# Two weight matrices transposed from DRAM, one load for the key, and an inverse Fourier table built by DMA, in a fused layer with its gradients

## The chip, the cores and the metric

The kernel runs on one core of a Trainium2 chip. Its time is the device time of one execution in microseconds (us). Times of several runs are given as a median with the smallest and the largest; a profile is taken from one further execution, whose own time is given beside them.

## The reference

The kernel computes a layer and all of its gradients in one launch. S = 2048 tokens, D = 512 channels, F = 1376 hidden units, all inputs bf16:

```python
def _A_ref(q, k, v, shift_k, ssm_k, ssm_D):      # q is xn here
    k_pad = jnp.pad(k, ((0, 0), (3, 0), (0, 0)))
    k_shift = sum(k_pad[:, t:t+S, :] * shift_k[:, 3-t] for t in range(4))
    kv = k_shift * v
    y  = irfft(rfft(kv, 2*S) * rfft(ssm_k, 2*S))[:S]   # long convolution, per channel
    return q * (y + kv * ssm_D)

def _B_ref(x, w_gate, w_up, w_down):
    return (sigmoid(x @ w_gate) * (x @ w_up)) @ w_down

xn  = layernorm(A_q)
out = A_q + _A_ref(xn, A_k, A_v, ...) * silu(_B_ref(xn, ...))
```

There are ten outputs: out, and with grad_out given the gradients of A_q, A_k, A_v, shift_k, ssm_k, ssm_D, w_gate, w_up and w_down. The input B_x is not used.

## The kernel before

*How the order of the work comes about.* The kernel is written as generators that record operations. A class `Rec` keeps every operation with its operands and dependences; a list scheduler (`order`, L347) then lays them out on the engines with a cost model (`cost` L290 for compute, `dcost` L327 for DMAs), and `emit` issues them in that order. All matmuls therefore have line L544 in the profile and everything else has L546. Each engine works its own list in order, and so do the queues: a DMA that is issued by SyncE (SP) goes to SP's queue, and the same holds for the queues of ScalarE (ACT) and GpSimd (POOL). Buffers are rings in one large SBUF slab (`Ring`, `Arena`), so in the profile nearly every on-chip buffer is called `slab`.

*Forward (about 0 to 208 us).* Three generators are interleaved. `strG` goes over 8 blocks of 256 tokens: load x (`f_x`), layer norm (`f_ln`), transpose of xn (`f_T`, a transposing DMA on SP; block 0 is transposed on TensorE instead), and the gate and up matmuls (`f_gen`), whose sigmoid and h are kept on chip for blocks 6 and 7 and written to DRAM scratch (`sF_d`, `hS_d`) for the others. `strK` transforms the filter ssm_k for four groups of 128 channels with a length-4096 FFT made of matmuls and twiddles. `strV` does, for each channel group, the 4-tap shift on the key as matmuls (`tok`) on a transposed key `kT`, the product with v, the forward FFT, the product with the filter's spectrum, and the inverse (`inv3`, `inv1`, ending in stream transposes on VectorE (DVE)).

The key comes transposed from DRAM in two loads of 256 columns (`ld_kT`, L905), the second recorded at the second channel group (L1009). Tables: `gen_fft_consts` (L576) makes the forward cosine table, a copy of it in DRAM scratch (`Cn_d`) and the twiddles; `gen_inv_table` (L631), called in the first channel group, makes the inverse table `Ci` with integer steps on DVE and two Sin on ACT. The row of shift_k (`skr`) is loaded in the beginning and spread over the partitions by four matmuls with a row of ones (`skb`, L944 to 947). `Dcol_b` (L926) and `skT` (L927) are small loads on ACT's queue that bring ssm_D and shift_k with the channel on the partition.

*Between the passes.* SP's list then holds the loads of w_down (`wd`), its transpose (`wdT`), and the transposes of gate and up:

```python
1071    nc.sync.dma_start_transpose(wdT[:, :, 0:F], B_w_down)
1073    for w, wT in ((wg, wgT), (wu, wuT)):
1074        for db in range(4):
1075            nc.sync.dma_start_transpose(wT[:, :, db * 128:(db + 1) * 128], w[:, db, :])
```

Gate and up are read from their copies in SBUF, 128 rows at a time; these copies are padded from 1376 to FP = 1408 columns with zeros, so a transposed weight has 11 blocks of 128 partitions.

*Backward over token blocks (about 208 to 365 us).* `stepB` (L1157) takes the blocks in the order 6, 7, 0 to 5. For each, `z_gen` (L1085) multiplies h by w_down, makes out and the gradient dz, and transposes dz by a DMA on SP (`dzT`); `d_gen` (L1117) multiplies dzT by `wdT` and makes the gradients of gate and up (`dg`, `du`, also written to scratch); `x_gen` (L1135) multiplies these by `wgT` and `wuT` and finishes the gradient through the layer norm. sigmoid and h of blocks 0 to 5 are loaded again on SP.

*The rest.* Weight gradients (L1195), then per channel group the backward of the long convolution (`frontC` L1247, `backC` L1261). In `backC` DVE makes dks, and two copies inside SBUF move its last rows to other partitions (the carried rows, L1290 and 1291, on POOL's queue) before the 4-tap shift is applied backwards.

Of the kernel before, what the change touches and what calls it, by code (L numbers as in the profile page):

```python
# [16 lines left out]
P = 128  # L17
# [9 lines left out]
NG = 4  # L27
# [135 lines left out]
class Rec:  # L163
# [163 lines left out]
    def dcost(self, alt):  # L327

        eng, meth, a, k = alt
        dst, src = a[0], a[1]  # L330
        nb = math.prod(dst.shape) * esize(dst.dtype)
        if "transpose" in meth:
            return (1.4 if str(src.space) != "DRAM" else nb / 260e3), nb / 256 * 18 / 16e3
        run = 4096 if eng == "sync" else 1 << 13
        for v in (dst, src):
            dims = [d for d in v.ap if d[1] > 1]
            r = 1
            for s, n in reversed(dims if str(v.space) == "DRAM" else [d for d in v.ap[1:] if d[1] > 1]):
                if s != r:
                    break  # L340
                r *= n
            run = min(run, r * esize(v.dtype))
        pk = nb / run
        d = pk * max(8 + 0.0375 * run, 18) / min(16, pk) / 1e3
        return (0.58 + max(0, pk - 256) * 3e-4 if eng == "gpsimd" else 0.36 + max(0, pk - 128) * 6e-4), d

    def order(self):  # L347
# [28 lines left out]
        pipe = {"gpsimd": 0.0, "hw": 0.0}  # L376
# [40 lines left out]
        while ndone < len(ops):  # L417
# [59 lines left out]
            if op.dma:  # L477
                occ, d = self.dcost(alt)
                me, other = ("gpsimd", "hw") if e == "gpsimd" else ("hw", "gpsimd")
                t = max(t, pipe[me] - 12.0)  # L480
                t0 = max(pipe[me], t + 1.5)
                share = min(d, max(0.0, pipe[other] - t0))
                pipe[me] = t0 + d + share
                if share:
                    pipe[other] += share
# [90 lines left out]
def gen_fft_consts(nc, ar, negpi, CN, TT, RT, I32, Cn_d):  # L576
# [8 lines left out]
    nc.gpsimd.iota(a, pattern=[[1, 16]], base=0, channel_multiplier=16)  # L585
    pi_ = tmp([4], i32)
    nc.gpsimd.iota(pi_[:, 0:1], pattern=[[0, 1]], base=0, channel_multiplier=1)
    b = tmp([64], i32)
    nc.gpsimd.iota(b, pattern=[[2, 64]], base=1, channel_multiplier=0)
# [9 lines left out]
    x32 = tmp([32], f32)  # L599
    nc.gpsimd.iota(x32, pattern=[[1, 32]], base=0, channel_multiplier=0, allow_small_or_imprecise_dtypes=True)  # L600
# [28 lines left out]


def gen_inv_table(nc, ar, negpi, Ci):  # L631
    rings = []

    def tmp(shape, dt):
        r = Ring(ar, shape, dt)
        rings.append(r)
        return r.ap
    pk = tmp([1], i32)
    for e in range(2):
        nc.gpsimd.iota(pk[64 * e:64 * e + 64], pattern=[[0, 1]], base=1, channel_multiplier=2)  # L640
    kf = tmp([1], f32)
    nc.vector.tensor_copy(kf, pk)
    nn, mc = tmp([16, 64], f32), tmp([2, 16, 64], i32)
    m = mc[:, 0]
    for h in range(2):
        nc.gpsimd.iota(nn, pattern=[[1, 16], [32, 64]], base=16 * h, channel_multiplier=0, allow_small_or_imprecise_dtypes=True)
        nc.vector.tensor_scalar(m, nn, kf[:, 0:1], None, ALU.mult)
        nc.vector.tensor_single_scalar(mc[:, 1], m, 8191, ALU.bitwise_and)
        nc.vector.tensor_single_scalar(m, m, 6144, ALU.add)
        nc.vector.tensor_single_scalar(mc[:, 0], m, 8191, ALU.bitwise_and)  # L650
        nc.scalar.activation(Ci[:, :, 16 * h:16 * h + 16], mc, ACT.Sin, bias=negpi, scale=2 * math.pi / 8192)
    for r in rings:
        r.free()
# [11 lines left out]
def kernel_impl(ctx, tc, A_q, A_k, A_v, A_shift_k, A_ssm_k, A_ssm_D, B_x, B_w_gate, B_w_up, B_w_down,  # L665
# [49 lines left out]
    Ci = Ring(ar, [2, 32, 64]).ap  # L715
# [32 lines left out]
    def f_T(q):  # L748
        T[q]["xnT"] = xnT_r.next()
        nc.sync.dma_start_transpose(T[q]["xnT"].rearrange("p t b k -> p (t b) k"),  # L750
                                    xnA[:, 2 * q:2 * q + 2, :].rearrange("p t d -> p (t d)"))

# [91 lines left out]
    def inv1(B, dst):  # L844
        for jh in range(2):
            ps = nc.ps("m2", [2, 8, 64], f32)
            calls = []
            for jj in range(8):
                j = 8 * jh + jj
                for c in range(2):  # L850
                    for r in range(2):
                        for e in range(2):
                            h = slice(64 * e, 64 * e + 64)
                            calls.append(("matmul", (ps[64 * r:64 * r + 64, e, jj], Ci[h, c, 16 * r + j, :],
                                                     B[h, c, 16 * r + j].rearrange("p u w -> p (u w)")),
                                          dict(start=(c == 0), stop=(c == 1))))
# [6 lines left out]
    def inv1n(B, dst):  # L863
        ps = nc.ps("f4", [32, 64], f32)
        for jh in range(2):
            for j8 in range(2):
                calls = []
                for jj in range(8 * j8, 8 * j8 + 8):
                    for c in range(2):
                        for e in range(2):  # L870
# [3 lines left out]
                                                     Ci[h, c, j, :]), dict(start=(c == 0), stop=(c == 1))))  # L874
# [120 lines left out]
    def strV():  # L995
        for cg in range(NG):
# [11 lines left out]
            if cg == 1:  # L1008
                ld_kT(1)  # L1009
# [5 lines left out]
            if cg == 0:  # L1015
                gen_inv_table(nc, ar2, negpi, Ci)
# [29 lines left out]

    CN_r.free()
    x2_r, go_r = Ring(ar, [2, D], n=2), Ring(ar, [2, D], n=2)
    dzT_r = Ring(ar, [2, 4, 128], n=2)
    dxa_r = Ring(ar, [2, D], n=2)  # L1050
    wd_r = Ring(ar, [NFB, D])
    zw = {k: Ring(ar, [2, D]) for k in ("sigz", "gate", "s_out", "dgate", "om")}
# [15 lines left out]
    nc.sync.dma_start(wd[0:96, NFB - 1, :], B_w_down[128 * (NFB - 1):F, :])  # L1068
    BQ = list(range(8 - NKEEP, 8)) + list(range(8 - NKEEP))
# [191 lines left out]
    def backC():  # L1261
        for cg in range(NG):
# [27 lines left out]
            nc.gpsimd.dma_start(dks[0:64, NJ:NJ + 3, :], dks[64:128, 0:3, :])  # L1290
            nc.gpsimd.dma_start(dks[64:127, NJ:NJ + 3, :], dks[1:64, 0:3, :])
# [53 lines left out]
    for r in [wd_r, x2_r] + list(zw.values()):  # L1345
# [97 lines left out]
```

## Time and profile before

| what | value |
|---|---|
| time, median of 3 runs (smallest to largest) | 586.28 us (585.12 to 590.41) |
| time of the profiled execution | 581.78 us |
| its span | 580.0 us |
| mean granted TensorE clock | 0.928 |
| PE busy | 485.9 us (84%), 6721 instructions |
| DVE busy | 409.9 us (71%), 625 |
| ACT busy | 273.2 us (47%), 335 |
| POOL busy | 51.9 us (9%), 92 |
| packets | 183,200, of which 112,607 under 512 bytes |
| SP's queue (q1), share of the 16 DMA engines' span | 66.4% |
| POOL's queue (q0) | 13.2% |
| ACT's queue (q10) | 0.1% |
| HBM read and written | 38.97 MB and 47.35 MB, 149 GB/s |

Engines: PE is TensorE's matmul, DVE VectorE, ACT ScalarE, POOL GpSimd, SP SyncE. Busy time counts neither register nor semaphore instructions nor the issuing of DMAs. The table of windows gives for each stretch of the span its length, the busy time of PE, its weight loads, DVE, ACT and POOL with the number of instructions in brackets, the granted TensorE clock, the busy share of the 16 DMA engines and GB/s. A line of the timeline gives start, length, engine, line and operation, output and input by the program's names, how many instructions run together in it, and in square brackets how long the engine stood idle before and what ended this. A line that begins with SPq is a DMA that SP issues.

### The profile page before, as it was taken

The numbers are of one execution on the slowest core, as the hardware profiler recorded it, in microseconds if no ns is written. First come the engines' busy times: TensorE is split into PE (matmuls) and PEld (weight loads), VectorE is DVE, ScalarE is ACT, GpSimd is POOL, SyncE is SP. The second block draws the span as 40 slices with busy tenths as digits, with TensorE's granted clock in tenths as the row PEclk, the third lists the DMA queues.
The fourth block names the chain that finished last, engine by engine and source line by source line (L and its number), as shares of the span: only waits on it lengthen the run. The fifth ranks groups of instructions, "written<-read, shape, count | busy, mean of one in ns | idle before, by whom it ended". The sixth has DMA issues, their size and how long they took to land. (4 is left out here: it accounts for less than half of the span.)

```text
span 580.0 us, 15280 instructions
## 1 busy us (share of the span) xinstructions
PE 485.9 (84%) x6721; PEld 304.7 (53%) x6721; DVE 409.9 (71%) x625; ACT 273.2 (47%) x335; POOL 51.9 (9%) x92
## 2 busy tenths in 40 slices
PE   4385979999599839999999999897687889669986
PEld 2283767887476615544564655343443444345444
DVE  5589988769448369779887698267674995566363
ACT  4369666767325423333453343355562451642412
POOL 6121341112111000000000000000000010000000
PEclk9697998999879878999999999899687899889999
DMA  8923698653949995587685869999569879998735
GB/s 244 278 73 135 197 225 252 186 193 127 258 110 257 234 213 129 172 252 203 188 225 152 254 140 233 247 267 222 164 164 192 177 204 280 231 247 174 178 95 149
DMA packets 183200, 114.93 MB, mean 198 GB/s; under 512 B 112607, under 2 KB 168637, under 8 KB 182110
## 3 DMA queue, kind: packets, MB, share of 16 engines
q1 hardware_dynamic: 175324, 88.59, 66.4%
q0 software_dynamic: 6752, 25.36, 13.2%
q8 instruction: 52, 0.85, 0.6%
q10 hardware_dynamic: 1058, 0.01, 0.1%
q14 instruction: 14, 0.11, 0.1%
HBM read 38.97 MB, written 47.35 MB: 149 GB/s over the span
## 5 line engine op out<-in xcount | busy, mean ns | idle before, releaser
L544 PE MATMUL psum<-slab 64*64 64x64 bf16 (+8 forms) x6712 | 483.5, 260 | 87.5 <-issue 23.7
L544 PEld LDWEIGHTS <-slab 128*128 128x128 bf16 (+6 forms) x6712 | 303.8, 105 | 267.5 <-issue 109.3
L546 ACT CAST slab<-psum 128x1024 bf16<-128x1024 f32 (+3 forms) x236 | 199.1, 891 | 198.1 <-PE psum L544 162.9
L546 DVE TENSOR_TENSOR slab<-slab 128x1024 bf16<-128x1024 bf16 (+4 forms) x317 | 247.9, 814 | 42.6 <-PE psum L544 16.2
L546 ACT ACTIVATE slab<-psum 128x1024 bf16<-128x1024 f32 (+2 forms) x56 | 49.0, 877 | 85.3 <-PE psum L544 76.8
L546 DVE CAST slab<-psum 128x1024 bf16<-128x1024 f32 (+2 forms) x39 | 41.3, 1067 | 46.8 <-ACT slab L546 34.0
L546 DVE SCALAR_TENSOR_TENSOR slab<-slab 128x512 bf16<-128x512 bf16 (+1 forms) x48 | 25.6, 532 | 22.6 <-ACT slab L546 21.9
L546 DVE TENSOR_TENSOR slab<-psum,slab 128x1024 bf16<-128x1024 f32 (+2 forms) x28 | 28.2, 1007 | 18.7 <-PE psum L544 15.8
L546 DVE STREAM_TRANSPOSE slab<-slab 128x512 f32<-128x512 f32 x48 | 31.0, 686 | 10.5 <-ACT slab L546 10.1
L546 DVE TENSOR_SCALAR slab<-slab 128x1 f32<-128x1 f32 (+10 forms) x74 | 28.2, 410 | 8.3 <-DMA slab<-slab 5.8
L546 ACT ACTIVATE slab<-slab 128x512 bf16<-128x512 bf16 (+2 forms) x20 | 19.4, 977 | 16.1 <-DVE slab L546 15.0
L546 POOL DMA_DIRECT2D slab<-slab x8 | 4.3, 544 | 190.8 <-DVE slab L546 190.8
L546 DVE BATCH_NORM_STATS2 slab<-slab 128x6 f32<-128x512 bf16 x16 | 11.0, 685 | 12.2 <-DMA slab<-in_A_q_dram 12.2
L546 POOL MEMSET slab<- 128x128 bf16 (+3 forms) x9 | 3.0, 342 | 166.5 <-issue 165.3
L546 POOL TENSOR_TENSOR slab<-slab 128x1 f32<-128x1 f32 (+1 forms) x20 | 11.4, 573 | 34.4 <-DVE slab L546 34.1
L546 POOL DMA_DIRECT2D KK_d<-slab x16 | 8.8, 547 | 52.1 <-ACT slab L546 45.4
L546 POOL DMA_DIRECT2D hS_d<-slab x8 | 8.8, 1102 | 25.8 <-DVE slab L546 22.9
L546 ACT ACT_TABLE_LOAD x7 | 9.0, 1283 | 3.4 <-issue 2.3
L546 POOL DMA_DIRECT2D sF_d<-slab x6 | 3.3, 550 | 29.3 <-ACT slab L546 28.9
L546 PE MATMUL psum<-slab 128*4 128x128 bf16 (+1 forms) x9 | 2.5, 437 | 2.3 <-DMA slab<-in_A_shift_k_dram 2.3
L546 POOL IOTA slab<- 64x1 int32 (+5 forms) x8 | 3.5, 460 | 2.1 <-DVE slab L546 2.0
L546 DVE BATCH_NORM_AGGREGATE slab<-slab 128x2 f32<-128x6 f32 x16 | 2.9, 180 | 0.5
(17 smaller groups left out, 18.8 us busy)
## 6 DMA issues: line engine op xcount, KB each, us to landing
out_dram<-slab SPq DMA_DIRECT2D x74, 128.0 KB, 3.3
KK_d<-slab POOLq DMA_DIRECT2D x16, 512.0 KB, 4.6
slab<-KK_d SPq DMA_DIRECT2D x8, 1024.0 KB, 6.6
hS_d<-slab POOLq DMA_DIRECT2D x8, 704.0 KB, 6.7
dgS_d<-slab SPq DMA_DIRECT2D x8, 704.0 KB
duS_d<-slab SPq DMA_DIRECT2D x8, 704.0 KB, 7.0
sF_d<-slab POOLq DMA_DIRECT2D x6, 704.0 KB, 4.4
slab<-sF_d SPq DMA_DIRECT2D x6, 704.0 KB, 7.8
```

The lines of the kernel that those rows point to most:

```text
L544: getattr(self.nc.tensor, m)(*[place(v) for v in aa], **{x: place(v) for x, v in kk.items()})
L546: getattr(getattr(self.nc, eng), meth)(*[place(v) for v in a], **{x: place(v) for x, v in k.items()})
```

## The change

It has these parts.

1. *Key.* `ld_kT` loads the whole key, 512 columns, in one transposing DMA, early; the two-buffer rings `dg4` and `acc` become single.
2. *Start.* The integer ramps of the forward tables are made first on POOL and the rest of the tables after the first layer norm; xn of blocks 0 and 1 is transposed on TensorE (`f_Tpe`); the first 512 columns of gate and up come on ACT's queue, the rest and v on POOL's.
3. *Inverse table.* `gen_inv_table` is gone. `Ci` is built from the forward table in DRAM scratch: one transposing load into `Ct`, then eight copies of 32 partitions, all on SP. Its layout changes, and with it the indices in the inverse matmuls.
4. *Row of shift_k.* Its load goes to POOL's queue at the end of the forward pass, and the four matmuls that spread it, with four copies on ACT, are recorded in `stepB` ahead of the third block. In the order as built the matmuls stand on PE ahead of `z_gen(7)`.
5. *Weights.* `wgT` and `wuT` are read transposed from the weights in DRAM: for each a memset of the padding, a transposing load of 1280 columns, and one `dma_start_transpose` for the last 96 columns. The program as built has for the first a transposing DMA instruction and for the second a plain copy, 96x512x1.
6. *Buffers and planner.* Some rings are allocated ahead of `CN_r.free()`. The planner's price of a transposing load from DRAM goes from 260 to 215 bytes per ns, and it keeps a third DMA pipe, for ACT's queue.
7. *Carried rows.* The two copies of each channel group are issued by ACT instead of POOL.

```diff
@@ dcost, order
-            return (1.4 if str(src.space) != "DRAM" else nb / 260e3), nb / 256 * 18 / 16e3
+            return (1.4 if str(src.space) != "DRAM" else nb / 215e3), nb / 256 * 18 / 16e3
...
-        pipe = {"gpsimd": 0.0, "hw": 0.0}
+        pipe = {"gpsimd": 0.0, "hw": 0.0, "act": 0.0}
...
@@ gen_fft_consts
+    b = tmp([64], i32)
+    nc.gpsimd.iota(b, pattern=[[2, 64]], base=1, channel_multiplier=0)
...
+    x32 = tmp([32], f32)
+    nc.gpsimd.iota(x32, pattern=[[1, 32]], base=0, channel_multiplier=0, allow_small_or_imprecise_dtypes=True)
+    yield
...
@@
-def gen_inv_table(nc, ar, negpi, Ci):
-    rings = []
-
-    def tmp(shape, dt):
-        r = Ring(ar, shape, dt)
-        rings.append(r)
-        return r.ap
-    pk = tmp([1], i32)
-    for e in range(2):
-        nc.gpsimd.iota(pk[64 * e:64 * e + 64], pattern=[[0, 1]], base=1, channel_multiplier=2)
-    kf = tmp([1], f32)
-    nc.vector.tensor_copy(kf, pk)
-    nn, mc = tmp([16, 64], f32), tmp([2, 16, 64], i32)
-    m = mc[:, 0]
-    for h in range(2):
-        nc.gpsimd.iota(nn, pattern=[[1, 16], [32, 64]], base=16 * h, channel_multiplier=0, allow_small_or_imprecise_dtypes=True)
-        nc.vector.tensor_scalar(m, nn, kf[:, 0:1], None, ALU.mult)
-        nc.vector.tensor_single_scalar(mc[:, 1], m, 8191, ALU.bitwise_and)
-        nc.vector.tensor_single_scalar(m, m, 6144, ALU.add)
-        nc.vector.tensor_single_scalar(mc[:, 0], m, 8191, ALU.bitwise_and)
-        nc.scalar.activation(Ci[:, :, 16 * h:16 * h + 16], mc, ACT.Sin, bias=negpi, scale=2 * math.pi / 8192)
-    for r in rings:
...
@@ buffers
-    Ci = Ring(ar, [2, 32, 64]).ap
+    Ci_m = Ring(ar, [2, 16, 128]).ap
+    Ci = Ci_m.rearrange("p c j (q r) -> p c r j q", r=2)
...
@@
+    def f_Tpe(q):
+        T[q]["xnT"] = xnT_r.next()
+        ps = nc.ps("m2", [8, 128], f32)
+        nc.burst("full", 8 * 0.056, [("matmul", (ps[:, 4 * t + db], xnA[:, 2 * q + t, db * 128:(db + 1) * 128], ident),
+                                      dict(start=True, stop=True)) for t in range(2) for db in range(4)])
+        nc.evac(T[q]["xnT"].rearrange("p t b k -> p (t b) k"), ps[:], 1024)
...
@@
-    kT_r = Ring(ar, [2, 16 + S], n=1)
-    dg4_r = Ring(ar, [4, GW], n=2)
+    dg4_r = Ring(ar, [4, GW])
     vg_r = Ring(ar, [NJ, 2 * GW])
-    acc_r = Ring(ar, [NJ, GW], n=2)
+    acc_r = Ring(ar, [NJ, GW])
...
@@
-    def ld_kT(cp):
-        kT = kT_r.next()
-        nc.gpsimd.memset(kT[:, :, 0:16], 0.0)
-        nc.sync.dma_start_transpose(kT[:, :, 16:16 + S], A_k[0][:, cp * 256:(cp + 1) * 256])
-        stA["kT", 2 * cp], stA["kT", 2 * cp + 1] = kT[:, 0], kT[:, 1]
+    def ld_kT():
+        kT = Ring(ar, [NG, 16 + S])
+        nc.gpsimd.memset(kT.ap[:, :, 0:16], 0.0)
+        nc.sync.dma_start_transpose(kT.ap[:, :, 16:16 + S], A_k[0])
+        for cg in range(NG):
+            stA["kT", cg] = kT.ap[:, cg]
+        return kT
...
@@
-    skr = ar.view(h_r.blks[1][0], [D * 4], bf16)[0:1, :]
-    ones1 = ar.view(sig_r.blks[1][0], [P], bf16)[0:1, :]
+    consts = gen_fft_consts(nc, ar2, negpi, CN, TT, RT, I32, Cn_d)
+    next(consts)
+
+    def ld_w(eng, f0, f1):
+        for w, src in ((wg, B_w_gate), (wu, B_w_up)):
+            eng.dma_start(w[:, :, f0:f1], src[:, f0:f1].rearrange("(db p) f -> p db f", p=P))
     f_x(0)
-
-    def ld_w(f0, f1):
-        for w, src in ((wg, B_w_gate), (wu, B_w_up)):
-            nc.gpsimd.dma_start(w[:, :, f0:f1], src[:, f0:f1].rearrange("(db p) f -> p db f", p=P))
-    ld_w(0, 512)
+    ld_w(nc.scalar, 0, 512)
+    make_identity(nc, ident)
+    f_x(1)
     ld_KT(0)
-    nc.scalar.dma_start(skr, A_shift_k.rearrange("(o d) t -> o (d t)", o=1))
     nc.scalar.dma_start(Dcol_b, A_ssm_D.rearrange("(cg p) -> p cg", p=P))
     nc.scalar.dma_start(skT, A_shift_k.rearrange("(cg p) t -> p cg t", p=P))
     nc.vector.memset(negpi, -math.pi)
     nc.vector.memset(neghalf, -0.5)
-    nc.vector.memset(ones1, 1.0)
-    make_identity(nc, ident)
-    f_x(1)
+    ld_w(nc.gpsimd, 512, 1024)
+    ld_w(nc.gpsimd, 1024, F)
+    kT_r = ld_kT()
+    ld_v(0, nc.gpsimd)
     f_ln(0)
-    T[0]["xnT"] = xnT_r.next()
-    ps = nc.ps("m2", [8, 128], f32)
-    nc.burst("full", 8 * 0.056, [("matmul", (ps[:, 4 * t + db], xnA[:, t, db * 128:(db + 1) * 128], ident),
-                                  dict(start=True, stop=True)) for t in range(2) for db in range(4)])
-    nc.evac(T[0]["xnT"].rearrange("p t b k -> p (t b) k"), ps[:], 1024)
-    ld_w(512, 1024)
-    ld_kT(0)
-    ld_w(1024, F)
-    ld_v(0, nc.gpsimd)
-    gen_fft_consts(nc, ar2, negpi, CN, TT, RT, I32, Cn_d)
-    for db in range(4):
-        pb = nc.ps("m1", [512], f32)
-        nc.tensor.matmul(pb[:], ones1, skr[:, db * 512:(db + 1) * 512], start=True, stop=True)
-        nc.scalar.copy(skb[:, :, db * 128:(db + 1) * 128], pb[:].rearrange("p (d t) -> p t d", t=4))
+    f_Tpe(0)
+    next(consts)
+    Ct_r = Ring(ar2, [16, P])
+    nc.sync.dma_start_transpose(Ct_r.ap, Cn_d.rearrange("p j k -> p (j k)"))
+    for h in range(2):
+        for c in range(2):
+            for e in range(2):
+                nc.sync.dma_start(Ci_m[64 * e + 32 * h:64 * e + 32 * h + 32, c], Ct_r.ap[64 * h + 32 * c:64 * h + 32 * c + 32])
+    Ct_r.free()
     nc.gpsimd.memset(wg[:, :, F:FP], 0.0)
...
@@
-                f_T(q + 1)
+                (f_Tpe if q == 0 else f_T)(q + 1)
...
@@ strV
-            if cg == 1:
-                ld_kT(1)
...
-            if cg == 0:
-                gen_inv_table(nc, ar2, negpi, Ci)
...
@@ between the passes
+    skr_r, ones_r = Ring(ar, [D * 4]), Ring(ar, [P])
+    skr, ones1 = skr_r.ap[0:1, :], ones_r.ap[0:1, :]
+    nc.gpsimd.dma_start(skr, A_shift_k.rearrange("(o d) t -> o (d t)", o=1))
+    nc.vector.memset(ones1, 1.0)
     BQ = list(range(8 - NKEEP, 8)) + list(range(8 - NKEEP))
     b_ld(BQ[0])
     nc.gpsimd.memset(wdT[:, :, F:FP], 0.0)
     nc.sync.dma_start_transpose(wdT[:, :, 0:F], B_w_down)
-    for w, wT in ((wg, wgT), (wu, wuT)):
-        for db in range(4):
-            nc.sync.dma_start_transpose(wT[:, :, db * 128:(db + 1) * 128], w[:, db, :])
+    for w, wT in ((B_w_gate, wgT), (B_w_up, wuT)):
+        nc.gpsimd.memset(wT[96:P, NFB - 1, :], 0.0)
+        nc.sync.dma_start_transpose(wT[:, 0:NFB - 1, :], w[:, 0:128 * (NFB - 1)])
+        nc.sync.dma_start_transpose(wT[0:96, NFB - 1, :], w[:, 128 * (NFB - 1):F])
...
@@ stepB
+            if n == 2:
+                for db in range(4):
+                    pb = nc.ps("m1", [512], f32)
+                    nc.tensor.matmul(pb[:], ones1, skr[:, db * 512:(db + 1) * 512], start=True, stop=True)
+                    nc.scalar.copy(skb[:, :, db * 128:(db + 1) * 128], pb[:].rearrange("p (d t) -> p t d", t=4))
...
@@ backC
-            nc.gpsimd.dma_start(dks[0:64, NJ:NJ + 3, :], dks[64:128, 0:3, :])
-            nc.gpsimd.dma_start(dks[64:127, NJ:NJ + 3, :], dks[1:64, 0:3, :])
+            nc.scalar.dma_start(dks[0:64, NJ:NJ + 3, :], dks[64:128, 0:3, :])
+            nc.scalar.dma_start(dks[64:127, NJ:NJ + 3, :], dks[1:64, 0:3, :])
```

More of the change, by code (lines that the diff above doesn't have):

```diff
@@ L478, in order @@
                 occ, d = self.dcost(alt)
-                me, other = ("gpsimd", "hw") if e == "gpsimd" else ("hw", "gpsimd")
+                me = {"gpsimd": "gpsimd", "scalar": "act"}.get(e, "hw")
                 t = max(t, pipe[me] - 12.0)
                 t0 = max(pipe[me], t + 1.5)
-                share = min(d, max(0.0, pipe[other] - t0))
+                share = 0.0
+                for other in pipe:
+                    if other != me:
+                        more = min(d, max(0.0, pipe[other] - t0))
+                        if more:
+                            pipe[other] += more
+                            share += more
                 pipe[me] = t0 + d + share
-                if share:
-                    pipe[other] += share
                 fin = pipe[me] + DSL
@@ L585, in gen_fft_consts @@
     nc.gpsimd.iota(a, pattern=[[1, 16]], base=0, channel_multiplier=16)
+    b = tmp([64], i32)
+    nc.gpsimd.iota(b, pattern=[[2, 64]], base=1, channel_multiplier=0)
     pi_ = tmp([4], i32)
     nc.gpsimd.iota(pi_[:, 0:1], pattern=[[0, 1]], base=0, channel_multiplier=1)
-    b = tmp([64], i32)
-    nc.gpsimd.iota(b, pattern=[[2, 64]], base=1, channel_multiplier=0)
+    x32 = tmp([32], f32)
+    nc.gpsimd.iota(x32, pattern=[[1, 32]], base=0, channel_multiplier=0, allow_small_or_imprecise_dtypes=True)
+    yield
     m = tmp([16, 64], i32)
@@ L598, in gen_fft_consts @@
     nc.scalar.activation(Cn, mc.rearrange("p j h c l -> p j (h c l)"), ACT.Sin, bias=negpi, scale=sc)
-    x32 = tmp([32], f32)
-    nc.gpsimd.iota(x32, pattern=[[1, 32]], base=0, channel_multiplier=0, allow_small_or_imprecise_dtypes=True)
     nc.vector.tensor_single_scalar(pi_[:, 1:2], pi_[:, 0:1], 31, ALU.bitwise_and)
@@ L628, in gen_fft_consts @@
         r.free()
-def gen_inv_table(nc, ar, negpi, Ci):
-    rings = []
-    def tmp(shape, dt):
-        r = Ring(ar, shape, dt)
-        rings.append(r)
-        return r.ap
-    pk = tmp([1], i32)
-    for e in range(2):
-        nc.gpsimd.iota(pk[64 * e:64 * e + 64], pattern=[[0, 1]], base=1, channel_multiplier=2)
-    kf = tmp([1], f32)
-    nc.vector.tensor_copy(kf, pk)
-    nn, mc = tmp([16, 64], f32), tmp([2, 16, 64], i32)
-    m = mc[:, 0]
-    for h in range(2):
-        nc.gpsimd.iota(nn, pattern=[[1, 16], [32, 64]], base=16 * h, channel_multiplier=0, allow_small_or_imprecise_dtypes=True)
-        nc.vector.tensor_scalar(m, nn, kf[:, 0:1], None, ALU.mult)
-        nc.vector.tensor_single_scalar(mc[:, 1], m, 8191, ALU.bitwise_and)
-        nc.vector.tensor_single_scalar(m, m, 6144, ALU.add)
-        nc.vector.tensor_single_scalar(mc[:, 0], m, 8191, ALU.bitwise_and)
-        nc.scalar.activation(Ci[:, :, 16 * h:16 * h + 16], mc, ACT.Sin, bias=negpi, scale=2 * math.pi / 8192)
-    for r in rings:
-        r.free()
+    yield
 def nview(ap3):
@@ L853, in inv1 @@
                             h = slice(64 * e, 64 * e + 64)
-                            calls.append(("matmul", (ps[64 * r:64 * r + 64, e, jj], Ci[h, c, 16 * r + j, :],
+                            calls.append(("matmul", (ps[64 * r:64 * r + 64, e, jj], Ci[h, c, r, j, :],
                                                      B[h, c, 16 * r + j].rearrange("p u w -> p (u w)")),
@@ L873, in inv1n @@
                             calls.append(("matmul", (ps[64 * e:64 * e + 64, j], B[h, c, j].rearrange("p u w -> p (u w)"),
-                                                     Ci[h, c, j, :]), dict(start=(c == 0), stop=(c == 1))))
+                                                     Ci[h, c, j // 16, j % 16, :]), dict(start=(c == 0), stop=(c == 1))))
                 nc.burst("64x64", 0.5, calls)
@@ L1044, in kernel_impl @@
         r.free()
+    x2_r, go_r = Ring(ar, [2, D], n=2), Ring(ar, [2, D], n=2)
+    wd_r = Ring(ar, [NFB, D])
+    zw = {k: Ring(ar, [2, D]) for k in ("sigz", "gate", "s_out", "dgate", "om")}
     CN_r.free()
-    x2_r, go_r = Ring(ar, [2, D], n=2), Ring(ar, [2, D], n=2)
     dzT_r = Ring(ar, [2, 4, 128], n=2)
     dxa_r = Ring(ar, [2, D], n=2)
-    wd_r = Ring(ar, [NFB, D])
-    zw = {k: Ring(ar, [2, D]) for k in ("sigz", "gate", "s_out", "dgate", "om")}
     wdT_r = Ring(ar, [4, FP])
@@ L1344, in kernel_impl @@
     live = run_streams([(gated(stepB(), "B"), 8 * 45056, 0.0, 1.0)], until=lambda: "z15" in flags)
-    for r in [wd_r, x2_r] + list(zw.values()):
+    for r in [wd_r, x2_r, skr_r, ones_r] + list(zw.values()):
         r.free()
```

## The prediction

> **What bounds the kernel now.** I read the table of windows first, cut at the edges of the stages, then the timeline around each stretch in which TensorE (PE) stands idle, and last the DMA view of short windows for the price of small packets.
>
> ```profile
> 0.00:26.65 26.65, 9.18 (x52) 5.94 (x53) 15.27 (x53) 11.30 (x12) 11.74 (x28) 0.86 0.95 258
> 42.00:62.50 20.50, 13.10 (x190) 7.95 (x188) 18.88 (x26) 16.77 (x15) 3.45 (x6) 0.75 0.46 156
> 207.60:216.30 8.70, 0.03 (x1) 0.06 (x2) 8.40 (x12) 1.94 (x2) 0.00 (x0) 0.66 0.87 243
> 216.30:365.00 148.70, 144.23 (x827) 81.12 (x828) 121.76 (x210) 60.82 (x85) 0.73 (x1) 0.99 0.74 193
> ```
>
> Columns after the length: busy time of PE, PE's weight loads, DVE, ACT, POOL, granted clock, DMA share, GB/s. The loop of the backward pass over token blocks (216 to 365) is bound by PE, busy 144.2 of 148.7 us, so whatever delays its beginning moves the end one for one. Ahead of it PE loses time in three places: the start (9.2 busy of 26.7), the stretch from 42 to 62 where DVE and ACT are nearly full, and a hole of 8.7 us between forward and backward.
>
> ```profile
> 5.23 16.52 SPq L546 DMA_TRANSPOSE slab<-in_A_k_dram  x1
> 26.65 12.35 PE L544 MATMUL psum<-slab 128*128 128x128 bf16 x152 [6.95 <-DMA slab<-in_A_k_dram]
> 175.74 1.28 DVE L546 STREAM_TRANSPOSE slab<-slab 128x512 f32<-128x512 f32 x2
> 175.89 6.80 SPq L546 DMA_TRANSPOSE slab<-in_B_w_down_dram  x1
> 182.87 23.90 SPq L546 DMA_TRANSPOSE slab<-slab  x8
> 207.03 0.90 DVE L546 TENSOR_SCALAR slab<-slab 128x2816 bf16<-128x2816 bf16 x1 [5.75 <-DMA slab<-slab]
> 213.09 1.26 SPq L546 DMA_TRANSPOSE slab<-slab  x1
> 216.27 5.95 PE L544 MATMUL psum<-slab 128*128 128x256 bf16 x33 [8.71 <-DMA slab<-slab]
> ```
>
> SyncE (SP) is one queue in order. It puts out wdT (175.89), then the eight transposes of gate and up (23.9 us), then the loads of block 0 and the transpose of dz for block 6 (213.09, landed 3.2 us later at 216.27), on which d_gen(6) and so PE wait. Whatever is put ahead of that transpose on SP delays the whole backward pass.
>
> **The tail of the new weight transposes.** The change reads gate and up transposed from DRAM: 1280 columns in one call and the last 96 in a second. In the program as built the first call is a transposing instruction, but the second is a plain copy of shape 96x512x1: its source steps 1376 elements from one element to the next, so nothing in it is contiguous for more than 2 bytes. That is 49,152 runs of 2 bytes, once for gate and once for up. The kernel before has one load of that kind: Dcol_b (L926), 512 lone elements on ACT's queue.
>
> ```profile
> q10 hardware_dynamic: 1058, 0.01, 0.1%
> DMA packets 509, 0.07 MB, mean 60 GB/s; under 512 B 477, under 2 KB 477, under 8 KB 509
> q10 hardware_dynamic: 464, 0.00, 22.0%
> q1 hardware_dynamic: 45, 0.07, 19.1%
> DMA packets 2044, 1.04 MB, mean 346 GB/s; under 512 B 18, under 2 KB 2044, under 8 KB 2044
> q1 hardware_dynamic: 2044, 1.04, 114.8%
> ```
>
> The first line is the page's: ACT's queue moved 0.01 MB in 1058 packets, so each lone element is a packet of its own (512 for Dcol_b, 512 for skT, few for the rest). The next three are the window 2.55 to 3.65 us, in which the elements of Dcol_b pass: 464 packets in 1.10 us, while they hold the 16 engines for 22.0%. Busy time of one is 0.22 x 1.10 x 16 / 464 = 8.3 ns, which over 16 engines is 0.52 ns per element: 25.7 us for a tail, the floor. They arrive, though, only every 1.10 us / 464 = 2.37 ns, on engines mostly idle; at that pace a tail takes 116 us, the ceiling. The last two lines (window 369.2 to 372.2, stores of 512-byte runs on SP's queue) show that SP can be supplied a packet every 3.0 us / 2044 = 1.47 ns with engines full. A partition's row has 4 runs in Dcol_b and 11 in those stores. If a row costs R and a run d, R + 4d = 9.5 and R + 11d <= 16.1 ns give d <= 0.95; a row of the tail has 512 runs, so 96 x (5.7 + 512 x 0.95) = 47 us at most. I take the middle of 25.7 and 47, **37 us for each tail**, since shape and queue type are those of Dcol_b and the row cost is the simplest reading of its slow arrival; 25.7 and 116 stay for the range.
>
> The Trainium skill speaks against this edit (DMA: Bandwidth & Descriptors, "Rules for kernel authors"): a strided last dimension is lowered to one descriptor per element, and a plain copy that transposes by its access pattern is put at 19 times the cost of the hardware transpose. The packets of Dcol_b agree with the first half. By the second, as an estimate from that section of the Trainium skill, a tail would be 9 us and the sum 3 us below the time before; no run here shows that factor.
>
> **The sum.**
> 1. *Start.* One transposing load of the whole key adds 4096 packets of 256 bytes; the wdT row gives 6.80 us / 5504 = 1.24 ns each, so 5.1 us: landing moves from 26.65 to about 31.7. In the built order PE has 220 matmuls ahead of the first use instead of its first few dozen: 124 of 256 columns at about 0.10 us (43.71: 24 in 2.26), 64 of 128 at 0.060 and 32 of 512 at 0.052, 17.9 us; before, PE did 9.18 - 1.86 (the four skr matmuls) = 7.3 us by its landing. So 10.6 us more work in 5.1 us more time: -5.5 us (bounds 0, if evacuations hold PE, and -7).
> 2. *Inverse table.* It leaves DVE (six int32 steps of 0.80 and two of about 1.2: 7.2 us) and ACT (two Sin of 2.0, four table loads of 1.28: 9.1 us), all in the window 42 to 62, where PE is idle 7.4 us. Other evacuations fill part of it: -3 (bounds 0 and -7.4). Its replacement, one transposing load and eight copies on SP, lies well ahead of inv1, its first reader, behind some 60 us of PE work; uncovered it would cost about 10 x 0.5 us of SP. The forward tables ahead of f_ln(0) delay that by 1.2 us (1.2 + 3 x 0.8 + 13 x 0.14 us of DVE after the first iota, against x landing at 5.78): +1.2. Stage together: **-7** (bounds +3, if the key lands later than its use, and -14).
> 3. *Between the passes.* wdT now waits for the last stream transposes, 177.0 before, so 170.0. SP: wdT 6.8 (176.8), gate 5120 packets x 1.24 = 6.3 (183.1), tail 37 (220.1), up 6.3 (226.4), tail 37 (263.4). Behind these stand, in order, the loads of sig and h for block 0 (1.41 MB at some 300 GB/s, 4.7 us), the dz transpose (3.2 us, as before), the out_0 stores, the next x: PE resumes at 271.3 instead of 216.3, **+55**, which holds the -7. The dg buffers no longer wait for SBUF transposes (the 5.75 us of DVE above), which gains nothing here: the later dz transpose is late instead. PE's four skr matmuls now stand ahead of z_gen(7) and wait for a 4 KB load on POOL; about 4 us (issue 0.55, landing as the carried rows' 4.5), hidden in that hole.
> 4. *Carried rows.* Eight copies go from POOL to ACT: 0.5 us of ACT each, and ACT now stands in order behind DVE's dks, its evacuations behind it. One of four visibly cost DVE 7.2 us (below). -2 (bounds +4: ACT 8 x 0.5 exposed; -7.2: that wait gone).
>
> ```profile
> 431.73 1.15 POOL L546 DMA_DIRECT2D slab<-slab  x2 [68.10 <-DVE slab L546]
> 443.32 13.37 DVE L546 TENSOR_TENSOR slab<-slab 128x2048 bf16<-128x2048 bf16 x14 [7.18 <-DMA slab<-slab]
> ```
>
> 55 - 2 = **+53 us**. The profiled execution took 581.78 (span 580.0, 1.8 around it), so it would take 635; the median of the runs, 586.28, is 4.5 above it, so 639. With the tails' bounds 25.7 and 47 alone: 617 and 659. In general the change is 2 x tail - 21 us; it breaks even at 10.5 us a tail, 0.21 ns per element.
>
> **Rivals.**
> - *Elements at the pace at which Dcol_b's arrive*, 2.37 ns: 116 us a tail, 586.3 + 232 - 21 = 797. For it: the only 2-byte packets in the trace, with engines 60% idle. Against: only 512 packets, and rows of 4 may pay a row cost that 512 spread out. Anything above 60 us a tail I count here (685 and up).
> - *The Trainium skill's factor* (a copy that strides costs 19 hardware transposes): 1376 KB in 6.80 us is 202 KB/us, a nineteenth is 10.6, 96 KB take 9 us: 586.3 + 18 - 21 = 583. Against: below the floor of 25.7 that the packets' busy time sets. It belongs to the Trainium skill's sentence above.
> - *The tail is merged into large packets* and takes about 1 us: then dz is ready when DVE is, the hole of 8.7 us goes, less the 4 us for skr now uncovered: -7 - 2 - 8.7 + 4 = -14, 573, faster. It decides below 0.21 ns per element. Against: 1058 packets for 9 KB.
>
> **Chances.** The forecast (tails of 25.7 to 60 us, 617 to 685) 0.52; slow elements 0.35; the Trainium skill's factor 0.05; merged 0.04; the rest (slower still) 0.04. The measurement tells about 1% from no change. Faster by over 1% is the merged case, 0.04; within 1% that of the factor 19, 0.05; slower, 0.91. The range 600 to 800 leaves out the two fast cases and what is slower still; the forecast's own is 617 to 685.
>
> **What would show it.** Right: two plain copies 96x512x1 on SP's queue, some 98,000 more packets under 512 B (112,607 before), SP held 25 us or more by each; a hole in PE of 50 to 70 us ended by a DMA slab<-slab, and the loop behind it as long as before (148.7). The wait of 6.95 for the key gone, the PE idle from 42 to 62 shorter, no int32 steps there. Wrong: packets of more than 2 bytes in the tails, dz's transpose overtaking them, or a hole under 20 us.

## The result and the profile after

The changed kernel takes 673.2 us (median of 4 runs, 667.67 to 677.79) against 585.7 us (581.64 to 590.41): a ratio of 1.149, 95% interval 1.133 to 1.165. Medians and ranges go by all runs of a kernel, ratios and their intervals by its faster runs alone. The profiled execution is the slowest of the four, 677.79 us; its span is 676.0, 96.0 more than before. The table of windows has the columns explained above. Its first two rows cover the same times as in the table before; the others are the hole, the loop over token blocks, and the backward convolution:

```profile
0.00:26.65 26.65, 12.05 (x99) 9.96 (x100) 16.85 (x51) 11.11 (x10) 9.63 (x24) 0.95 1.02 268
42.00:62.50 20.50, 19.10 (x319) 15.96 (x316) 18.65 (x27) 15.87 (x18) 5.30 (x9) 1.00 0.96 248
203.50:324.23 120.73, 0.00 (x0) 0.00 (x1) 7.54 (x10) 2.85 (x3) 0.00 (x0) 0.52 1.75 29
324.23:477.13 152.90, 147.23 (x841) 82.27 (x842) 114.09 (x201) 61.25 (x87) 0.00 (x0) 0.99 0.76 196
477.13:676.00 198.87, 169.57 (x3264) 92.32 (x3264) 130.76 (x170) 90.28 (x117) 0.73 (x1) 0.94 0.94 209
```

For 120.7 us TensorE does nothing, while the DMA engines are full (share 1.75) and move 29 GB/s. Before, the loop to the first matmul on the `Cn_d` tables and the stage behind it read:

```profile
216.27:369.17 152.90, 147.12 (x838) 82.12 (x839) 123.26 (x214) 62.32 (x88) 0.73 (x1) 0.99 0.75 195
369.17:580.00 210.83, 174.59 (x3267) 93.25 (x3267) 132.29 (x171) 89.43 (x117) 5.07 (x9) 0.92 0.89 199
```

The loop is 152.90 us in both. So the 96.0 us are +108.0 up to where the loop begins (324.23 against 216.27) and -12.0 in the last stage (198.87 against 210.83).

The timeline of SP and of TensorE shows what fills the hole (the two DMA_DIRECT2D from the weights are the tails):

```profile
160.99 5.68 SPq L550 DMA_TRANSPOSE slab<-in_B_w_down_dram  x1
167.29 11.25 SPq L550 DMA_TRANSPOSE slab<-in_B_w_gate_dram  x1
178.60 0.70 SPq L550 DMA_DIRECT2D slab<-in_B_w_gate_dram  x1
179.48 75.28 SPq L550 DMA_TRANSPOSE slab<-in_B_w_up_dram  x1
254.92 0.60 SPq L550 DMA_DIRECT2D slab<-in_B_w_up_dram  x1
255.64 58.20 SPq L550 DMA_DIRECT2D slab<-sF_d  x1
315.38 6.08 SPq L550 DMA_TRANSPOSE slab<-slab  x1
194.03 1.86 PE L550 MATMUL psum<-slab 1*128 1x512 bf16 x4 [9.37 <-DMA slab<-in_A_shift_k_dram]
324.23 5.93 PE L548 MATMUL psum<-slab 128*128 128x256 bf16 x35 [120.81 <-DMA slab<-slab]
```

Issuing a tail takes SP 0.6 to 0.7 us. The next DMA behind each is held, for 75.28 and 58.20 us, and the transpose of dz, for which TensorE waits, is issued only at 315.38. The page of the profile counts 210,850 packets under 512 bytes, 98,243 more than before. Ten microseconds in the middle of the up tail (276 to 286), in the DMA view:

```profile
DMA packets 8344, 0.02 MB, mean 2 GB/s; under 512 B 8344, under 2 KB 8344, under 8 KB 8344
q1 hardware_dynamic: 8344, 0.02, 194.4%
```

One packet every 1.20 ns: 59 us for 49,152 of them. The share of 194% says that an engine has about two packets under way at once, so each lasts 1.944 x 10 us x 16 / 8344 = 37 ns, against 8.3 ns for an element of `Dcol_b` before.

### The profile page after: what moved, and what is told of

It reads as the page before. It is cut to its first block, busy times and chain, and to the rows that moved or that the text cites. A ratio compares the mean times of both kernels' runs of the same rounds, so it can differ in the third digit from the quotient of the medians.

```text
span 676.0 us, 15273 instructions
## 1 busy us (share of the span) xinstructions
PE 477.5 (71%) x6729; PEld 301.0 (45%) x6729; DVE 399.6 (59%) x612; ACT 269.1 (40%) x333; POOL 44.5 (7%) x80
## 2 busy tenths in 40 slices
DMA packets 282846, 116.17 MB, mean 172 GB/s; under 512 B 210850, under 2 KB 268412, under 8 KB 281756
## 5 line engine op out<-in xcount | busy, mean ns | idle before, releaser
L548 PE MATMUL psum<-slab 128*128 128x256 bf16 (+8 forms) x6720 | 475.2, 256 | 186.0 <-DMA slab<-slab 124.3
L548 PEld LDWEIGHTS <-slab 128*128 128x128 bf16 (+5 forms) x6720 | 300.1, 104 | 361.2 <-DMA slab<-slab 126.8
L550 DVE TENSOR_TENSOR slab<-slab 128x1024 bf16<-128x1024 bf16 (+5 forms) x317 | 248.4, 814 | 166.3 <-ACT slab L550 126.6
L550 ACT CAST slab<-psum 128x1024 bf16<-128x1024 f32 (+2 forms) x241 | 205.0, 899 | 294.6 <-PE psum L548 241.8
L550 DVE CAST slab<-psum 128x1024 bf16<-128x1024 f32 (+2 forms) x35 | 35.1, 1008 | 49.4 <-ACT slab L550 17.2
L550 DVE TENSOR_SCALAR slab<-slab 128x1 f32<-128x1 f32 (+7 forms) x66 | 22.9, 383 | 1.9 <-DMA dgS_d<-slab 0.6
L550 ACT ACTIVATE slab<-slab 128x512 bf16<-128x512 bf16 (+2 forms) x18 | 15.6, 864 | 18.2 <-DVE slab L550 17.0
L550 DVE BATCH_NORM_STATS2 slab<-slab 128x6 f32<-128x512 bf16 x16 | 10.9, 683 | 0.8 <-DMA slab<-in_A_q_dram 0.8
L550 ACT ACTIVATION_READ_ACCUMULATOR slab<-psum 128x1 f32 x16 | 3.1, 194 | 0.0
```

What stands on the lines that cost most here:

```text
L548: getattr(self.nc.tensor, m)(*[place(v) for v in aa], **{x: place(v) for x, v in kk.items()})
L550: getattr(getattr(self.nc, eng), meth)(*[place(v) for v in a], **{x: place(v) for x, v in k.items()})
```

## The experiments

**The tails as the cause of the hole.** In `tails_2cols`, `half_tails`, `pace`, `tails_2cols_carry_pool` and `tail_sbuf_pinned` the plan of the changed kernel is kept: in their traces TensorE has the same 6729 matmuls in the same order of shapes. What is issued at the place of a tail differs, where a tail is cut short the memset ahead of it zeroes the whole last block, and in the last two the queue of the carried rows differs too. The cuts of code below are abridged.

```diff
-        nc.sync.dma_start_transpose(wT[0:96, NFB - 1, :], w[:, 128 * (NFB - 1):F])
+        nc.sync.dma_start_transpose(wT[0:96, NFB - 1, 0:2], w[0:2, 128 * (NFB - 1):F])   # at emission, same plan
```

> The tails copy only 2 of 512 columns (192 elements each, the rest of these rows left at zero); every engine keeps the order of the change. My theory: the tails are the whole loss, TensorE goes on without a hole (203.5 instead of 324.2), and what the change gains elsewhere, about 20 us ahead of the hole and 12 us in the backward convolution, is real: 672 - 120 = 552 us. Rival: the 12 us behind the loop came from the rest that TensorE had in the hole (mean granted clock 0.94 there against 0.92 before) and go with it: 564 us or more. Rival: the tails hide another wait of tens of us: over 575 us.

558.4 us (556.7 to 559.6), 0.956 of before (0.951 to 0.960). The tails are more than the whole loss. The backward convolution is still short with no long rest ahead of it, so the rest is not what shortened it. The 552 took the hole of the profiled execution from the median; from that execution's own 677.8 it is 557, and the profiled execution here took 556.7. What the hole had hidden shows now, the wait for the row of shift_k:

```profile
195.79 1.86 PE L556 MATMUL psum<-slab 1*128 1x512 bf16 x4 [10.94 <-DMA slab<-in_A_shift_k_dram]
197.58 45.56 PE L549 MATMUL psum<-slab 128*128 128x512 bf16 x246
355.16:554.90 199.74, 169.30 (x3264) 92.30 (x3264) 130.92 (x171) 90.00 (x117) 0.73 (x1) 0.94 0.92 208
```

(The first two lines are TensorE's timeline, the third the window of the last stage.) TensorE waits 10.9 us for 4 KB, and then runs from `z_gen(7)` into the loop without a hole.

**The weight part alone.** The kernel before, with lines 1073 to 1075 replaced by those of the change:

> The kernel before with the weight part of the change alone (transposes from DRAM and plain copies for the tails), TensorE's order almost that of before. wdT starts there at 175.9 us; from wdT's start to the end of the hole the changed kernel takes 324.2 - 161.0 = 163 us, so TensorE goes on at about 339 instead of 216.3: +123, some 707 us. Then the other parts of the change together are worth 35 us, which the tails hid. Rival: the other parts are worth nothing and the hole is shorter by itself here: 672 us.

705.8 us (693.0 to 719.1), 1.215 (1.202 to 1.228). In the trace, of the slowest of its runs, the DMAs behind the two tails are held on SP for 73.3 and 61.3 us, and TensorE has a hole of the same kind. The first of these DMAs and the end of the hole:

```profile
209.09 73.30 SPq L546 DMA_TRANSPOSE slab<-in_B_w_up_dram  x1
353.41 41.83 PE L544 MATMUL psum<-slab 128*128 128x256 bf16 x224 [138.34 <-DMA slab<-slab]
```

The estimate of 707 holds for the median: the other parts of the change together are worth 705.8 - 673.2 = some 33 us (25 by the fastest run of each), of which the prediction had 9 (-7 for the start and the table, -2 for the carried rows).

**What sets the price of a tail.** The edits in words:

```diff
-    gate: w[:, 1280:1376] -> wT[0:96, 10, :]      up: the same        (96 rows of 512 each)
+    half_tails   gate: 48 rows of 512             up: 96 rows of 256
+    pace         gate: 48 rows of 512, columns 28 apart    up: 16 rows of 512
```

> Both tails cut to half their elements, gate to 48 rows of 512, up to 96 rows of 256; the other half of the tails is left at zero, the order of all engines is that of the change. Per-element theory (1.22 ns for each 2-byte packet, read from 8,100 packets per 10 us in the hole of the trace): both last 30 us, the time falls by 60 us to about 612 us. Per-row theory (a price for each destination row, 60 / 96 = 0.62 us): gate 30, up stays at 60, about 642 us.

627.9 us (625.2 to 634.1): between the two theories, and neither holds, since equal numbers of elements went at unequal pace. The DMA view of half_tails at 206 to 212 (48 rows) and at 246 to 256 (96 rows):

```profile
DMA packets 2911, 0.01 MB, mean 1 GB/s; under 512 B 2911, under 2 KB 2911, under 8 KB 2911
q1 hardware_dynamic: 2911, 0.01, 196.9%
DMA packets 8468, 0.02 MB, mean 2 GB/s; under 512 B 8468, under 2 KB 8468, under 8 KB 8468
q1 hardware_dynamic: 8468, 0.02, 194.3%
```

That is 2.06 ns a packet with 48 rows and 1.18 ns with 96, although the rows of the 96 are half as long.

> Order of the change; the gate tail copies 48 columns that lie 28 apart (rows of 512 elements; wrong columns, which leaves a wrong block in the weight), the up tail copies 16 neighbouring columns (rows of 512); the rest of both blocks is zero. In half_tails 48 neighbouring rows of 512 went at 1.95 ns a packet (48 us), 96 rows of 256 at 1.1 ns (26 us), so the price is neither one per element nor one per row. Theory S: rows go side by side and the length of a row sets the time, about 0.1 us for each of its elements: 48 spread rows again 48 us, 16 rows again some 48 us. Theory L: reads of the same small piece of DRAM go one after another, and neighbouring columns share pieces: spread rows go much faster (under 25 us), 16 neighbouring rows at 3 to 4 ns a packet, about 30 us. Theory N: a fixed price per packet, whatever the shape: half_tails speaks against it; 8,192 packets would take 10 to 16 us.

618.3 us, one run. The same view of pace at 210 to 220 (48 spread rows) and at 252 to 258 (16 rows):

```profile
DMA packets 4818, 0.01 MB, mean 1 GB/s; under 512 B 4818, under 2 KB 4818, under 8 KB 4818
q1 hardware_dynamic: 4818, 0.01, 197.0%
DMA packets 2877, 0.01 MB, mean 1 GB/s; under 512 B 2877, under 2 KB 2877, under 8 KB 2877
q1 hardware_dynamic: 2877, 0.01, 197.1%
```

Spread columns go at the pace of neighbouring ones, 2.08 ns, so theory L falls. Sixteen rows of 512 pass in about 13 us (246 to 258.5), not 48, so theory S falls too. Theory N has the right time for them but not one price: 2.1 ns with 16 or 48 rows, 1.2 with 96. Why 96 rows go faster stays open. In every shape the engines hold about two packets each, and each takes 37 to 66 ns for 2 bytes.

**Tails without small packets.** `tail_sbuf` takes the last block from the weights' copies in SBUF, `tail_pe` from four matmuls with the identity; in both the planner lays out all the work anew. `tail_sbuf_pinned` issues the transposes of tail_sbuf at the place of the tails in the plan of the change, with the carried rows on GpSimd's queue.

```diff
-        nc.sync.dma_start_transpose(wT[0:96, NFB - 1, :], w[:, 128 * (NFB - 1):F])
+        for db in range(4):        # tail_sbuf; ws is the weight's copy in SBUF
+            nc.sync.dma_start_transpose(wT[:, NFB - 1, db * 128:(db + 1) * 128], ws[:, db, 128 * (NFB - 1):FP])
+        # tail_pe: instead four matmuls of ws[:, db, 1280:1408] with ident into PSUM, and nc.evac to wT[:, NFB - 1, :]
```

> The tails come from the weights' copies in SBUF by four transposing DMAs of 128x128 each instead of a plain copy; nothing is left out, the planner orders anew. Two groups of four at about 1.5 us replace 120 us. My theory: 672 - 108 = 564 us or a little less, faster than before the change by 3 to 5%. Rival: the eight small transposes wait on the queue as the eight large ones of the kernel before did (23.9 us), and the hole between the passes stays at 10 us: 570 us or more.

> Nothing is left out: the last block of each transposed weight is made by four TensorE matmuls with the identity from the weight's copy in SBUF and one evacuation, instead of the plain copy. SP's queue loses the two tails and gains nothing; TensorE gains 1 us. Theory: as tails_2cols, 556 to 562 us, with the wait for the row of shift_k (10.9 us there) as the largest one left between the passes. Rival: the planner's new order costs what tail_sbuf paid, 567 us or more.

> Nothing is left out: the order of tails_2cols_carry_pool on every engine, with each tail put out as four transposing DMAs of 128x128 from the weight's copy in SBUF at the place of the plain copy, carried rows on GpSimd's queue. SP is held by the eight small transposes for about 10 us ahead of the transpose of dz, of which some 5 us reach TensorE: 556 + 5 = 561 us, about 4% faster than before and 7 us faster than tail_sbuf and tail_pe, whose orders the planner made anew. Rival: the order is worth nothing and it ends at 568 to 570 us as those two.

569.6 us (567.1 to 576.6), 0.974 (0.968 to 0.979); 568.1 (563.7 to 573.4), 0.975 (0.966 to 0.984); and 562.1 (554.6 to 575.3), 0.959 (0.954 to 0.964). The last is the fastest that leaves nothing out, 4% below the kernel before. In tail_sbuf the two groups of four take SP 5.2 and 4.9 us, where the DMAs behind the plain copies were held for 133. Its 569.6 is above the 564 of the theory and near the 570 of the rival. tail_pe missed its 556 to 562: in the profiled executions its loop begins at 208.6, takes 154.5 us, and the last stage 202.9, against 205.3 (the end of `z_gen(7)`), 149.9 and 199.7 in tails_2cols. tail_sbuf_pinned, with the order of the change, came at the 561 that was expected.

**The row of shift_k.** `tail_pe_skr` is tail_pe with its load and its four matmuls at the start again.

> As tail_pe, with the row of shift_k loaded and spread at the start as before the change. My theory: the wait of 11 us goes, but dz of block 6 comes next, at most some 4 us earlier than now: 0 to 5 us faster than tail_pe, and the start loses about 2 us of TensorE. Rival: the whole 11 us are gained, about 547 us. Rival: the start pays as much as the hole gains: the same time.

575.0 us (571.8 to 579.9), slower than tail_pe, which no theory had. In the profiled executions (567.8 and 579.9, the slowest of its ten) the loop begins 7.2 us earlier (201.4 against 208.6), but the last stage grows. Its window in tail_pe and in tail_pe_skr:

```profile
363.09:566.00 202.91, 168.31 (x3268) 90.46 (x3268) 134.23 (x173) 87.41 (x115) 0.73 (x1) 0.96 0.89 204
355.41:578.10 222.69, 179.14 (x3268) 101.32 (x3268) 136.17 (x174) 86.30 (x114) 0.73 (x1) 0.85 0.81 187
```

The stage with the same number of matmuls takes 19.8 us longer. Their busy time is 10.8 us more, at a granted clock of 0.85 instead of 0.96. TensorE's order of that stage differs between the two traces; that the order is what lowered the clock is not shown.

**What shortened the backward convolution.** Three single edits: ACT as issuer alone against GpSimd in one plan (`tails_2cols_carry_pool`), the copies planned on ACT in the kernel before (`before_act`), and the planner's prices in the kernel before (`before_planner`).

```diff
+                if op.n in self.swap: eng = "gpsimd"       # tails_2cols_carry_pool: at emission, same plan
-            nc.gpsimd.dma_start(dks[...]                   # before_act, both copies
+            nc.scalar.dma_start(dks[...]
-            return (1.4 if str(src.space) != "DRAM" else nb / 260e3), ...    # before_planner, with the third pipe
+            return (1.4 if str(src.space) != "DRAM" else nb / 215e3), ...
```

> As tails_2cols, with the eight carried-row copies issued by GpSimd's queue as before the change, at the same place in an otherwise equal order. If ScalarE's queue is what made the backward convolution 12 us shorter, it is 7 to 12 us slower than tails_2cols. If the new order of the planner made it, or the rest, within 3 us of it.

> The kernel before with its eight carried-row copies recorded for ScalarE's queue, as the change does, and nothing else; the planner then lays out the backward convolution anew. In all kernels with the order of the change that stage (first matmul on the Cn_d tables to the end) took 194 to 200 us, in those with the order of before 211, whichever queue issued the copies. Theory A: planning the copies on ScalarE is what made that order: the stage falls to about 199 us and the time to some 573 us. Theory B: the order came from the planner's new prices or from what precedes: 580 to 586 us, stage at 208 to 213.

> The kernel before with only the planner's edits (215 instead of 260 for a transposing load from DRAM, a third DMA pipe for ScalarE's queue); no instruction is added or removed, the order changes on all engines. Theory B: the new prices make the better order of the backward convolution: stage at 199 us, some 572 us. Theory A: stage unchanged at 208 to 213 us, the time within 1% of before, unless the order elsewhere gets worse.

556.3 us (548.8 to 559.8), within 3 us of tails_2cols; 587.4 (585.3 to 589.2), 1.007 (1.004 to 1.010); 587.9 (582.9 to 593.8; the profiled execution took 592.4), 1.005 (1.001 to 1.009). The windows of the last stage in this order:

```profile
352.83:547.00 194.17, 167.45 (x3264) 91.80 (x3264) 130.54 (x170) 90.12 (x117) 5.00 (x9) 0.94 0.95 214
370.05:585.70 215.65, 175.85 (x3267) 96.68 (x3267) 130.88 (x170) 90.39 (x118) 0.73 (x1) 0.90 0.86 195
372.51:590.60 218.09, 176.46 (x3265) 95.95 (x3265) 130.92 (x169) 89.68 (x119) 5.09 (x9) 0.88 0.86 193
```

Neither the queue nor either edit alone makes the stage short; in before_act and before_planner it grew, which none of their theories had. What goes with its length is the order: TensorE's matmuls of that stage come in one and the same order of shapes in the traces of the changed kernel, of the five that keep its plan and of inv_engines below (194 to 200 us), in another in before and before_wT (211 in both), and in others again in the remaining five (203 to 223). tail_sbuf and tail_pe keep the buffers, the prices and the queues of the change and still have 203 to 204 us, so these parts alone do not make the stage short. Which decision in the plan does is not shown, and no part of the diff has the 12 us for itself.

**The inverse table.** `inv_engines` is tails_2cols with `gen_inv_table` back and the nine DMAs gone.

> As tails_2cols (tails of 2 columns, rest zero), but the inverse table is made on VectorE and ScalarE as before the change, the nine DMAs that built it gone. My price in the prediction: 3 us of the first 62.5 us (bounds 0 and 7.4): TensorE, busy 46.5 us of these in the changed kernel, would be at about 43, and the kernel 3 us slower than tails_2cols, 561 us, if the planner's order later stays as good. Rival: the DMAs delay the loads of x and the gain is nothing: 46 us busy, the same time.

559.6 us (556.2 to 562.1), the same as tails_2cols. The windows of the first 62.5 us and of what follows up to 149, first tails_2cols, then inv_engines:

```profile
0.00:62.50 62.50, 46.35 (x604) 38.82 (x604) 46.85 (x95) 34.80 (x36) 19.09 (x40) 0.97 1.03 259
62.50:149.00 86.50, 72.02 (x1483) 58.99 (x1476) 67.69 (x99) 58.86 (x66) 17.47 (x29) 0.98 0.67 206
0.00:62.50 62.50, 40.42 (x417) 33.00 (x418) 47.89 (x100) 34.73 (x32) 19.70 (x41) 0.86 0.79 208
62.50:149.00 86.50, 77.28 (x1590) 64.71 (x1588) 73.06 (x102) 65.04 (x73) 19.45 (x32) 1.00 0.69 217
```

In busy time TensorE is 5.9 us behind at 62.5 (3 were expected) and 0.7 behind at 149 (117.7 against 118.4): most of what the start loses is made up later in the stage. In matmuls done it is still behind there (2007 against 2087). wdT is issued 3.6 us later (162.47 against 158.84), and the loop's first matmuls come 1.2 us later (198.76 against 197.58), since both kernels wait there for the row of shift_k.

## Why the prediction was right, and where it was off

The forecast was slower, 639 us with 617 to 685 for its own case; 673 lies in it, and the mechanism is the one described: two plain copies of 49,152 elements on SP's queue, ahead of the transpose of dz. That the number fell inside the range is in part luck, as the sum at the end of this section shows.

- *The tails* were the term mis-sized: 37 us each, measured 59 at the steady pace of 1.20 ns a packet (the packets of gate's tail are spread over 65 us of the trace, those of up's over 59; tails_2cols, which drops nearly all of both, is 115 us faster). The step that failed is "a row costs R and a run d", fitted to `Dcol_b` and to 512-byte stores. It gave at most 47 us; the "ceiling" of 116 held, the "floor" of 25.7 rested on 8.3 ns a packet, which in a long copy became 37 to 66. A nearer row was in the same text: the 256-byte packets of the key and of wdT pass every 1.24 ns, and at that price a tail is 61 us. That the two agree may be chance, since 48 or 16 rows pass at 2.1 ns, nearer the 2.37 of the rival with slow elements.
- *The Trainium skill* (DMA: Bandwidth & Descriptors, "Rules for kernel authors") was right on one descriptor per element: 98,243 more packets. The Trainium skill's factor 19 is too mild here: as an estimate by the 202 KB/us of wdT, the hardware transpose of 96 KB would take 0.48 us, and the copy took 59, about 120 times as long.
- *Start and inverse table*, -7 us: wdT was issued at 160.99, not at the predicted 170.0, so 14.9 us earlier than before (175.89). Up to one and the same burst of inverse matmuls (160.39 before, 144.27 after) TensorE was idle 40.8 us before and 31.3 after: 9.5 less, near the 7.3 predicted. Missing in the sum was its busy time: 119.6 against 113.0. 1.9 of this are the four skr matmuls, which moved. In the first 62.5 us the granted clock rose from 0.84 to 0.97, and in inv_engines it is 0.86, so the rise goes with the table. How much of the shorter busy time the clock makes is not shown. inv_engines puts the table's share at 3.6 us at wdT, near the 3 priced, and near nothing at the end. One trace does not settle the size: in the six kernels with this order wdT goes out between 158.2 and 169.8, and in before, before_wT and before_act, which have one order up to there, between 175.1 and 181.5.
- *Behind the tails* 7.9 us were predicted from the end of the tail to TensorE; 10.3 were measured (313.96 to 324.23).
- *The skr matmuls*: predicted hidden in the hole, with about 4 us of load. Hidden they were; but the load took 8.7 us from issue to landing, and TensorE waited 9.4 us for it, 10.9 in tails_2cols, where it is the largest wait between the passes.
- *Carried rows*, -2 us: the stage fell by 12.0, but tails_2cols_carry_pool shows that the queue gains nothing. The gain goes with the plan of the stage, which the sum left out.

Together, in the two profiled executions: wdT 9.0 us earlier than predicted; from its issue to the end of the up tail 153.0 us instead of 93.4, of which the two tails make 2 x 22 = 44 and the three large transposes the rest (153 - 2 x 59 = 35 instead of 19.4; tails_2cols has 33.7 from wdT's issue to that of sF, so most of this is there without the tails); 2.4 behind them; 10.0 less in the last stage. -9.0 + 59.6 + 2.4 - 10.0 = 43, the difference between the 96 measured and the 53 of the sum. The terms that were too small come to 62 us and would by themselves have put the time at 639 + 62 = 701, outside the range; the start and the last stage, which gained 19 us more than foreseen, brought it back. The upper end of 685 stands for tails of 60 us, and they came at 59.

## What to carry to other kernels

Price a strided copy by its packets, and do not take the busy time of a few lone ones for the pace of a long copy: 8.3 ns became 37 to 66. The pace of the smallest packets that the trace shows in bulk was a better guide here (1.24 ns against 1.20), but it too would have been off for 48 rows (2.1). Look up what each transposing call becomes in the program as built: here the remainder of 96 columns became a plain copy, while 1280 columns became the transposing instruction. Remove a large stall only with the next wait in view: behind the tails stood a load of 4 KB that cost 11 us. Where a planner lays out the order, a part of a diff can move stages that it doesn't touch: keep the plan fixed and change what is issued, to learn what an edit is worth.

## What the runs showed of the hardware

- Long copies of 2-byte elements hold about two packets per DMA engine (share 194 to 197%) and pass one every 1.2 ns with 96 destination rows, every 2.1 ns with 48 or 16, whether the source columns are neighbours or 56 bytes apart.
- They begin fast and then slow down: with 16 rows 2,709 packets passed from 246 to 248, 1,458 in the next 2 us and 958 to 960 in each 2 us after that.
- The 3268 matmuls of the last stage ran at a granted clock of 0.96 in tail_pe and of 0.85, in another order, in tail_pe_skr, and took 168.3 and 179.1 us of busy time.
- With one order of TensorE's matmuls, the last stage took 194 to 200 us in seven kernels; with other orders 203 to 223.
